# Holding back the third expert's search, moving half of a conversion to ScalarE, and pairing the experts in another way

## The chip, the cores and the metric

The kernel runs on one core of one Trainium2 chip. The metric is the device time of one execution in microseconds, the median of three runs. The core has five engines with a queue of instructions each: TensorE (PE) multiplies matrices, VectorE (DVE), ScalarE (ACT) and GpSimd (POOL) work on tiles in on-chip memory, and SyncE (SP) issues most transfers. Each queue runs in the order in which the program wrote it; an instruction that waits holds up all that is behind it on its engine.

## The reference

Three steps in a row: attention over 4 x 8 heads of 576 tokens, a layer of eight experts to which tokens are assigned by their scores, and one dense layer with a squared ReLU.

```python
# attention: causal, with a bias from cumulated s; x is its output, 2304 tokens x 512
# experts: cap = 288 tokens each
logits = x @ w_gate
order = np.argsort(-logits.flatten())
for idx in order:                      # best scores first
    tok, e = idx // E, idx % E
    if assigned[tok] >= 0 or counts[e] >= cap:
        continue
    assigned[tok] = e
    counts[e] += 1
for e in range(E):
    mask = assigned == e
    out[mask] = np.maximum(x[mask] @ w1[e], 0.0) @ w2[e]
# dense layer, 512 -> 2048 -> 512, its weights given in float64
h = np.maximum(out @ w_in, 0.0)
y = h * h @ w_out
```

## The kernel before

**Stages.** Attention runs first (to about 230 us). Then the eight experts are found one after the other. Each of eight searches (`route_phases`, one phase for each expert) finds by counting the threshold at which an expert has its 288 tokens, and then the tokens' numbers (`idxs`). A search is a chain of small steps between VectorE and TensorE: VectorE compares (`wide`, L573), TensorE counts (L690, L697), VectorE reads the count (`ev` L694, `ge` L703), TensorE spreads the answer (L706). At its end TensorE makes the indices (L770), and GpSimd gathers the expert's rows (`rows`, L1023).

**Experts and layers.** Expert `e` has two kinds of blocks on TensorE, eight of each: kind 1 (`h` from w1, then `hH` on ScalarE, `hL` on VectorE) and kind 2 (`acc`, from w2), twelve matmuls of 288 columns each. `CHUNKS` groups the experts; behind the last expert of a chunk its dense layers run, 16 blocks each of kind 3 (`h` from w_in, then `s`, `sH` on ScalarE, `s` squared on VectorE, `sL` on GpSimd) and kind 4 (`acc`, w_out). A pair has matmuls of 512 columns, a single expert has half the columns in kind 3 and half the matmuls in kind 4. All products are made of three matmuls of high and low parts; so each weight is split, `wH` on ScalarE and `wL` on GpSimd or VectorE (L990, L993), three blocks ahead (`LS`). At the end of a chunk GpSimd scatters the output rows (L1229), 128 at a time.

**Conversion.** w_in and w_out come as float64. `Convert` makes float32 of 128 columns at a time: `begin` makes the exponent and mantissa (`ex`; for w_in, n of 16 and above, on ScalarE, L862) and one 16-bit half of `sg` (L877, on VectorE), `begin2` the other half (L877), `end` puts them together (L888, VectorE). There is one buffer `sg`, three of `ex` and three of the raw words. All of w_out is converted beside attention, three pieces of w_in are begun in the first search, and the others, in every second block from block 18 on (`CV0`, `CVM`): they are needed from the first chunk's layers on. Converted pieces are split into `winH` (ScalarE) and `winL` (GpSimd).

**Order.** The loop over `order` in `experts` writes all queues by hand. After each block `wait` goes down by the block's cost (1.0 for an expert's block, 1.7 for a pair's layer block, 0.9 for a single expert's); once it is at or below zero one search step is written and `wait` rises by the step's weight times `YS` (0.5, up to the second expert's search) or `YL` (1.3, from then on). Block 16 is the first of the second expert. Rows of an expert that is second in its pair are gathered at once when its indices are there; rows of others one block after another.

Of the kernel before, what the change touches and what calls it, by code (L numbers as in the profile page):

```python
# [6 lines left out]
FT = mybir.dt.float32  # L7
# [3 lines left out]
U16 = mybir.dt.uint16  # L11
AF = mybir.ActivationFunctionType
OP = mybir.AluOpType
# [458 lines left out]
NTOK, DM, E_, F1, F2 = 2304, 512, 8, 1024, 2048  # L472
# [113 lines left out]
def route_begin(tc, cn, L):  # L586
    V = tc.nc.vector
    alive = cn.rp.tile([128, NT], FT, name="alive", bufs=1)
    V.memset(alive, 1.0)
    for b in range(B):  # L590
        V.memset(alive[64:128, 5 * b:5 * b + 1], 0.0)
    cn.alive = alive

    cn.wide = cn.rp.tile([128, 64 * NT], BF, name="wide", bufs=1)
    tc.nc.gpsimd.memset(cn.wide, 0.0)

    cn.oh = cn.rp.tile([128, GT * NG, 8], BF, name="oh", bufs=1)
    V.memset(cn.oh, 0.0)
    cn.front = Front(tc, cn, L, alive)
# [188 lines left out]

NB1, NB2 = F1 // 128, F2 // 128

CHUNKS = [[0, 1], [2, 3], [4, 5], [6], [7]]
LASTC = len(CHUNKS) - 1
W20 = 'SV'
W2X = 'SV'
# [2 lines left out]
RS = 1  # L797
# [6 lines left out]
YS = 0.5  # L804
GD = 1
GS = 2
YL = 1.3
ML = 3
RF = 8
GE = 2  # L810
# [12 lines left out]
class Convert:  # L823
# [25 lines left out]
    def begin(self, pool=False):  # L849
        n = self.begun  # L850
        if n >= self.loaded:
            return
        self.begun += 1
        hw = self.r64[n][:, :, :, 1]
        ex = self.cn.cv.tile([128, 4, 128], FT, name="ex", bufs=3)
        sg = self.cn.cv.tile([128, 4, 128], I32, name="sg", bufs=1)

        if pool:
            self.nc.gpsimd.tensor_tensor(ex, hw.bitcast(FT), self.cn.m112[:, :, None].to_broadcast([128, 4, 128]),
                                         op=OP.mult)  # L860
        else:
            self.nc.scalar.activation(ex, hw.bitcast(FT), AF.Copy, scale=2.0 ** -112)  # L862
        self.half(n, sg, 0, 13, OP.logical_shift_right)
        self.ex[n] = (ex, sg)

    def begin2(self):
        n = self.begun - 1
        if n < 0 or n in self.two:
            return
        self.two.add(n)  # L870
        self.half(n, self.ex[n][1], 1, 32768, OP.bitwise_and)

    def half(self, n, sg, k, x, op):

        u = self.r64[n].rearrange("p c f w -> p (c f w)").bitcast(U16).rearrange("p (f w) -> p f w", w=4)
        o = sg.rearrange("p c f -> p (c f)").bitcast(U16).rearrange("p (f w) -> p f w", w=2)
        self.nc.vector.tensor_scalar(o[:, :, k], u[:, :, 2 * k + 1], x, None, op0=op)  # L877

    def end(self):
        n = self.done  # L880
# [43 lines left out]
def early_pools(tc, cn, L, win, wout):  # L924

    nc = tc.nc
    pools = []

    def pool(name, bufs, **kw):
        p = tc.tile_pool(name=name, bufs=bufs, **kw)  # L930
        pools.append(p)
        return p.__enter__()

    cn.rp = pool("m_rt", 2)
    cn.cv = pool("m_cv", 2)
    fx = pool("m_cf", 1)
    cn.woutR = fx.tile([128, NB2, DM], FT, name="woutR")
    cn.m112 = fx.tile([128, 1], FT, name="m112")
    nc.vector.memset(cn.m112, 2.0 ** -112)
    route_begin(tc, cn, L)  # L940
    cn.conv = Convert(tc, cn, win, wout)
    return pools


def experts(tc, cn, L, xd, w1, w2, win, wout, out):
    nc = tc.nc
# [3 lines left out]
    def pool(name, bufs, **kw):  # L950
        p = tc.tile_pool(name=name, bufs=bufs, **kw)
        pools.append(p)
        return p.__enter__()
# [3 lines left out]
    fx = pool("m_fix", 1)  # L957
# [43 lines left out]
    eids, idxs = [], []  # L1001
    route = route_phases(tc, cn, L, cn.rp, rps, eids, idxs)
    wait = [0]

    def route_step():
        l0 = len(idxs)
        y = next(route, 0)

        return y
# [37 lines left out]
    def w_load(blk):  # L1047
        k, e, f = blk
        if k == 1:
            RAWS[blk] = raw(w1[bass.ds(ereg(e), 1)].rearrange("e (c p) f -> p (e c) f", p=128)  # L1050
                            [:, :, 128 * f:128 * f + 128])
        elif k == 2:
            RAWS[blk] = raw(w2[bass.ds(ereg(e), 1), 128 * f:128 * f + 128, :].rearrange("e p (c d) -> (e p) c d", c=4))

    def w_split(blk):
        k, e, f = blk
        if k in (1, 2):
            W[blk] = split(RAWS.pop(blk), "SG" if k == 1 else (W2X if e else W20))
        elif k == 4:
            W[blk] = split(woutR[:, f, :].rearrange("p (c d) -> p c d", c=4), WO if e else WO0)  # L1060
# [8 lines left out]
    def block(blk, mid=lambda: None):  # L1069
# [10 lines left out]
        elif k == 3:  # L1080
# [6 lines left out]
            h = ps.tile([128, 512], FT, name="h", bufs=2)  # L1087
            if len(CHUNKS[e]) == 2:

                o, yh, yl = h.rearrange("p (a n) -> p a n", a=2), *(  # L1090
                    y.rearrange("p d (a n) -> p d a n", a=2)[:, :, :, :256] for y in (yh, yl))
            else:
                o, yh, yl = h[:, :n], yh[:, :, :n], yl[:, :, :n]
            if f == 0 and len(CHUNKS[e]) == 2:

# [56 lines left out]
    def post2(e, a):  # L1152
        c = min(n for n, es in enumerate(CHUNKS) if e in es)
        off = CAP * CHUNKS[c].index(e)
        if c not in Y:
            ytile(c)
        yh, yl = (t[:, :, off:off + CAP] for t in Y[c])
        for d in range(4):
            S.activation(yh[:, d, :], a[d][:, :CAP], AF.Copy)
            V.tensor_tensor(yl[:, d, :], a[d][:, :CAP], f32(yh[:, d, :]), op=OP.subtract)  # L1160
        n = (e + 1) % E_
        V.tensor_copy(idxR[32 * (n % 4):32 * (n % 4) + 32, n // 4:n // 4 + 1], idxs[e][0:32, 2:3])
        if e not in CHUNKS[0] and e < E_ - 1:
            keep(e)

    def keep(e):
        c = min(n for n, es in enumerate(CHUNKS) if e in es)
        o = CAP * CHUNKS[c].index(e) + 256
        for r, y in zip(R, Y[c]):
            G.tensor_copy(r[:, :, 32 * e:32 * e + 32], y[:, :, o:o + 32])  # L1170
# [97 lines left out]
    while not idxs:  # L1268
        y = route_step()
# [13 lines left out]
    def need(e):  # L1283
        if lw[0] is None:
            xrows(99)
            late_stores(nc, cn, 0)
            cn.otp.__exit__(None, None, None)
            lw[0] = pool("m_lw", 2, side="right")
        while len(idxs) <= e:

            route_step()
        if e not in gathered:
            gathered.add(e)
            if e and [e - 1, e] in CHUNKS:

                for c in range(3):
                    gather(e, c)
                soon.extend((xt, (e, d), 0) for d in range(4))
                return
            for c in range(3):  # L1300
                if e >= GE:
                    gathers.append((e, c, at[0] + GD + GS * c))
                else:
                    gather(e, c)
            for d in range(4):
                side.append((xt, (e, d), at[0] + (GD + 2 * GS if e >= GE else 0) + SD))
# [33 lines left out]
    for n, blk in enumerate(order):  # L1340
        at[0] = n
        routed = False
        while nl < min(len(order), n + LD + 1):
            if order[nl][0] in (1, 2):
                need(order[nl][1])
            w_load(order[nl])
            nl += 1
        while ns < min(len(order), n + LS + 1):
            w_split(order[ns])
            ns += 1  # L1350
        if blk[0] == 1:
            while any(a[0] == blk[1] for f, a, _ in soon):
                xt(*soon.popleft()[1])
            while any(f is xt and a[0] == blk[1] for f, a, _ in side):
                side_step()

        block(blk, mid if len(idxs) < 2 else lambda: None)
        seen.add(blk)
        wait[0] -= cost(blk)
        turn = blk[0] == 2 and blk[2] == NB1 - 1 and (blk[1] < TE or len(idxs) == E_)  # L1360
        if turn:
            flush()
        if len(idxs) < E_ and wait[0] <= 0 and n >= RS:
            wait[0] += route_step() * (YL if len(idxs) > 1 else YS)
            routed = True
        flush()
        if conv.done < 2 * NB2 and n % CVM == CVO and n >= CV0:
            conv_step()
        while gathers and gathers[0][2] <= n:
            gather(*gathers.popleft()[:2])  # L1370

        k, e, f = blk
        if k > 2:
            e = CHUNKS[e][-1]
        for _ in range(2):
            if soon and (1, soon[0][1][0] - 1, NB1 - 1) in seen:
                xt(*soon.popleft()[1])
        for _ in range(1 if len(idxs) < E_ else SW):
            if side and side[0][2] + (0 if routed or len(idxs) == E_ else SL) <= n and not (
                    side[0][0] is xt and side[0][1][0] and (1, side[0][1][0] - 1, NB1 - 1) not in seen):  # L1380
                side_step()
        if k > 1 and e + 1 < E_ and len(idxs) > e + 1:
            need(e + 1)
# [50 lines left out]
```

## Time and profile before

| | us |
|---|---|
| median of three runs | 965.55 (965.05 to 967.3) |
| profiled execution, device time | 963.51 |
| its span, first to last instruction | 961.7 |
| TensorE busy | 898.0 |
| VectorE busy | 575.1 |
| ScalarE busy | 455.8 |
| GpSimd busy | 405.7 |

By the trace the stages lie as follows, in us from the span's start: attention to 230, first search 230 to 269, experts 0 and 1 from 269.5 to 346.6, layers of the pair 0 and 1 to 451.3, experts 2 and 3 to 514.8, their layers to 612.8, experts 4 and 5 to 674.4, their layers to 766, expert 6 to 792.1, its layers to 837.4, expert 7 to 864.3, its layers and the last stores to the end. Times below are read in these stages: the busy time of an engine in a stretch, and the waits, which name the engine that sat idle and the instruction that ended its idle time.

### The profile page before, as it was taken

To read this page: it belongs to the slowest core of one execution; us is meant where nothing else is said; L and a number is where in the kernel's file an instruction comes from. 1 tells how busy PE (TensorE), PEld (TensorE's weight loads), DVE (VectorE), ACT (ScalarE), POOL (GpSimd) and SP (SyncE) were. 2 spreads that over 40 slices of the span, in tenths; PEclk is the share of its full clock that TensorE was granted. 3 is DMA by queue.
4 is the path that set the end of the run, shared out by engine and by line. 5 is a ranking of instruction groups with operands and counts; after the bars stand their busy time and mean duration, and the time that the engine had idled before them with its cause. 6 is when DMAs were issued, how large, how long until landed. Compare 5 with 4: busy or idle time off the path is not lost.

```text
span 961.7 us, 16567 instructions
## 1 busy us (share of the span) xinstructions
PE 898.0 (93%) x5836; PEld 733.9 (76%) x5836; DVE 575.1 (60%) x1517; ACT 455.8 (47%) x1055; POOL 405.7 (42%) x330
## 2 busy tenths in 40 slices
PE   4999999998688798999999999989999999999996
PEld 3676767776478786777898777889888899898885
DVE  7787888887867988734756444756432344442222
ACT  6677767775334554233353233443432455553321
POOL 4454554443523656646442321633323454533233
PEclk9999999999589999999999999999999999999999
DMA  6877696733634632101641100455000160140001
GB/s 169 212 175 191 152 241 169 189 96 124 202 104 136 204 103 77 33 1 45 208 133 44 33 1 1 136 150 164 13 1 1 49 204 1 29 137 1 0 1 45
DMA packets 73971, 95.54 MB, mean 99 GB/s; under 512 B 8128, under 2 KB 53184, under 8 KB 73888
## 3 DMA queue, kind: packets, MB, share of 16 engines
q1 hardware_dynamic: 68560, 79.93, 30.4%
q0 software_dynamic: 3360, 11.01, 3.4%
q10 hardware_dynamic: 1968, 3.54, 1.0%
q8 instruction: 46, 0.75, 0.3%
q14 instruction: 37, 0.30, 0.1%
HBM read 80.31 MB, written 9.44 MB: 93 GB/s over the span
## 4 chain that ended last, share of the span: by engine, by line
PE 74%; DVE 14%; issue 4%; DMA 4%; POOL 2%; ACT 2%; SPq 0%; DVEq 0%; POOLq 0%; ACTq 0%
PE h L1065 10%; PE h L1067 9%; PE h L1066 9%; PE acc L1113 6%; PE acc L1114 6%; PE acc L1115 6%; PE av L271 5%; PE pt L244 5%; PE acc L1065 3%; PE acc L1067 3%; PE acc L1066 3%; PE sc L199 3%; DVE sg L877 2%; DVE Q L168 2%; PE sc L200 2%
## 5 line engine op out<-in xcount | busy, mean ns | idle before, releaser
L1180 POOL TENSOR_TENSOR sL<-s,sH 128x512 fp32r<-128x512 f32 (+1 forms) x80 | 111.6, 1394 | 252.0 <-DVE s L1179 245.3
L1175 ACT ACTIVATE s<-h 128x512 f32<-128x512 f32 (+1 forms) x80 | 44.5, 556 | 220.7 <-PE h L1067 220.6
L1179 DVE TENSOR_TENSOR s<-s 128x512 f32<-128x512 f32 (+1 forms) x80 | 53.3, 667 | 153.0 <-ACT sH L1178 152.8
L993 POOL TENSOR_TENSOR wL<-raw,wH 128x512 fp32r<-128x512 f32 x64 | 83.5, 1312 | 98.4 <-ACT wH L990 96.2
L1065 PE MATMUL h<-yH,winH 128*128 128x512 f32 (+1 forms) x332 | 124.1, 374 | 0.0
L1067 PE MATMUL h<-yH,winL 128*128 128x512 f32 (+1 forms) x332 | 121.2, 365 | 0.0
L1066 PE MATMUL h<-yL,winH 128*128 128x512 f32 (+1 forms) x332 | 121.0, 364 | 0.0
L1113 PE MATMUL acc<-wH,sH 128*128 128x512 f32 x288 | 116.3, 404 | 0.0
L990 ACT ACTIVATE wH<-raw 128x512 fp32r<-128x512 f32 x128 | 80.2, 629 | 76.0 <-DMA raw<-in_w 39.8
L1114 PE MATMUL acc<-wL,sH 128*128 128x512 f32 x288 | 113.5, 394 | 0.0
L1115 PE MATMUL acc<-wH,sL 128*128 128x512 f32 x288 | 113.5, 394 | 0.0
L227 ACT ACTIVATE e<-sc,nm 128x576 f32<-128x576 f32 (+4 forms) x160 | 84.1, 526 | 48.1 <-DVE junk L216 41.4
L216 DVE TENSOR_SCALAR_CACHE_REDUCE junk<-sc 128x576 bf16<-128x576 f32 (+4 forms) x160 | 77.6, 485 | 34.0 <-PE sc L202 25.7
L244 PE MATMUL pt<-ident,e 128*128 128x128 f32 x448 | 81.4, 288 | 5.3 <-ACT e L227 4.8
L199 PE MATMUL sc<-K,Q 128*128 128x288 f32 (+2 forms) x192 | 74.0, 390 | 10.5 <-DVE Q L152 10.5
L1065 PE MATMUL h<-xH,wH 128*128 128x288 f32 x256 | 81.0, 316 | 2.7 <-DVE hL L1143 2.7
L1065 PE MATMUL acc<-hH,wH 128*128 128x288 f32 x256 | 79.1, 309 | 0.0
L1066 PE MATMUL h<-xL,wH 128*128 128x288 f32 x256 | 77.0, 301 | 0.0
L1067 PE MATMUL h<-xH,wL 128*128 128x288 f32 x256 | 76.4, 299 | 0.1
L1067 PE MATMUL acc<-hH,wL 128*128 128x288 f32 x256 | 75.8, 296 | 0.0
L1066 PE MATMUL acc<-hL,wH 128*128 128x288 f32 x256 | 75.7, 296 | 0.0
L160 POOL TENSOR_TENSOR K<-k,K 64x1152 fp32r<-64x1152 f32 x15 | 39.7, 2648 | 78.8 <-DMA q<-in_qT 21.9
(225 smaller groups left out, 2107.4 us busy)
## 6 DMA issues: line engine op xcount, KB each, us to landing
raw<-in_w SPq DMA_DIRECT2D x128, 256.0 KB
k<-in_kT SPq DMA_DIRECT2D x30, 288.0 KB
q<-in_qT SPq DMA_DIRECT2D x30, 288.0 KB
r<-in_wout SPq DMA_DIRECT2D x16, 512.0 KB
r<-in_win SPq DMA_DIRECT2D x16, 512.0 KB
vb<-in_vm SPq DMA_DIRECT2D x16, 256.0 KB
Q<-Q SPq DMA_DIRECT2D x8, 288.0 KB
QB<-Q SPq DMA_DIRECT2D x7, 288.0 KB
```

The source lines that it names most:

```text
L199: nc.tensor.matmul(o, Q1[:, a, c0:c0 + 128], K1[:, a, x0:x1], start=True, stop=False)
L227: nc.scalar.activation(o, v, AF.Exp, bias=nm[:m], scale=0.125, accum_out=sums[b % 2][:m, i, hd % H:hd % H + 1])
L244: nc.tensor.transpose(pt[:, j, :m], (E4[hd % 2] if i == 4 else E[i])[:m, 128 * j:128 * j + 128], cn.ident[:m, :m])
L990: S.activation(hi, src, AF.Copy)
L993: (G if eng[1] == "G" else V).tensor_tensor(lo, src, f32(hi), op=OP.subtract)
L1065: T.matmul(o, wh, xh, start=first, stop=False)
L1066: T.matmul(o, wh, xl, start=False, stop=False)
L1067: T.matmul(o, wl, xh, start=False, stop=last)
L1113: T.matmul(o, hi[:, c0:c0 + 128], wh, start=f == 0, stop=False)
L1114: T.matmul(o, hi[:, c0:c0 + 128], wl, start=False, stop=False)
L1115: T.matmul(o, lo[:, c0:c0 + 128], wh, start=False, stop=f == NB2 - 1)
L1180: G.tensor_tensor(lo, s, f32(hi), op=OP.subtract)
```

## The change

Four things change. The chunks are `[0, 1], [2], [3, 4], [5, 6], [7]` in place of `[0, 1], [2, 3], [4, 5], [6], [7]`. The third expert's search (two sets of indices are there) isn't written before block 26 (`R2`), in the middle of the second expert, and `wait` doesn't sink below -1. The weight of a search step is taken from a table, 1.2 and 1.25 in place of 1.3. And of the conversion of w_in one half of `sg` is made on ScalarE, as a product with 2^-13 and an added constant whose rounding gives the shift.

```diff
-CHUNKS = [[0, 1], [2, 3], [4, 5], [6], [7]]
+CHUNKS = [[0, 1], [2], [3, 4], [5, 6], [7]]
...
-YL = 1.3
+YY = [0, 0.5, 1.2, 1.2, 1.2, 1.25, 1.25, 1.25]
+R2 = 26
...
-        self.half(n, sg, 0, 13, OP.logical_shift_right)
+        o, u = self.halves(n, sg)
+        if n < NB2:
+            self.nc.vector.tensor_scalar(o[:, :, 0], u[:, :, 1], 13, None, op0=OP.logical_shift_right)
+        else:
+
+            self.nc.scalar.activation(o[:, :, 0], u[:, :, 1], AF.Identity, bias=self.cn.mhalf, scale=2.0 ** -13)
...
-        self.half(n, self.ex[n][1], 1, 32768, OP.bitwise_and)
...
+        o, u = self.halves(n, self.ex[n][1])
+        self.nc.vector.tensor_scalar(o[:, :, 1], u[:, :, 3], 32768, None, op0=OP.bitwise_and)
...
+    nc.vector.memset(cn.mhalf, -0.5 + 2.0 ** -14)
...
-        if len(idxs) < E_ and wait[0] <= 0 and n >= RS:
-            wait[0] += route_step() * (YL if len(idxs) > 1 else YS)
+        if len(idxs) < E_ and wait[0] <= 0 and n >= (R2 if len(idxs) == 2 else RS):
+            y = YY[len(idxs)]
+            wait[0] = max(wait[0], -1.0) + route_step() * y
```

The lines below the new ones move by 6 to 9: L862 becomes L863, L888 becomes L894, L993 becomes L1001, L1023 becomes L1031, L1143 becomes L1151, L1229 becomes L1237.

VectorE's queue in the second expert, beside its conversions; first before, with pieces of the third search (`k2f`, `wide`, `base`, `ev`, `ge`) between them:

```order
L573 TENSOR_TENSOR wide<-thr,k2f 128x840
L678 SCALAR_TENSOR_TENSOR base<-mi,base 128x1
L1143 SCALAR_TENSOR_TENSOR hL<-h,hH 128x288
L888 SCALAR_TENSOR_TENSOR ex<-ex,sg 128x512
L877 TENSOR_SCALAR sg<-r_4453 128x512 x2
L993 TENSOR_TENSOR wL<-raw,wH 128x512
L1143 SCALAR_TENSOR_TENSOR hL<-h,hH 128x288
L888 SCALAR_TENSOR_TENSOR ex<-ex,sg 128x512
L877 TENSOR_SCALAR sg<-r_4518 128x512 x2
L694 CAST ev<-mi 128x24
L993 TENSOR_TENSOR wL<-raw,wH 128x512
L703 TENSOR_SCALAR ge,some<-mi 42x8
```

and after:

```order
L1151 SCALAR_TENSOR_TENSOR hL<-h,hH 128x288
L894 SCALAR_TENSOR_TENSOR ex<-ex,sg 128x512
L878 TENSOR_SCALAR sg<-r_3394 128x512
L1001 TENSOR_TENSOR wL<-raw,wH 128x512
L1151 SCALAR_TENSOR_TENSOR hL<-h,hH 128x288
L894 SCALAR_TENSOR_TENSOR ex<-ex,sg 128x512
L878 TENSOR_SCALAR sg<-r_3527 128x512
L1001 TENSOR_TENSOR wL<-raw,wH 128x512
```

One L878 stands where two L877 stood, and for four conversions no search row stands between them.

ScalarE's queue at the same place after the change (`r` are the raw words):

```order
L1150 ACTIVATE hH<-h 128x288
L998 ACTIVATE winH<-ex 128x4x128
L863 ACTIVATE ex<-r_3527 128x512
L869 ACTIVATE sg<-r_3527,mhalf 128x512
L998 ACTIVATE wH<-raw 128x512 x2
L1150 ACTIVATE hH<-h 128x288
```

L869 is new in each such group of two blocks; the other rows stood there before too.

GpSimd's queue behind the layers of the first pair, where the third expert begins; before:

```order
L1229 DMA out<-r_5749,idx 2304x512
L1228 MEMSET spacer 1x1
L1229 DMA out<-ex,idx 2304x512
L993 TENSOR_TENSOR wL<-raw,wH 128x512
L1228 MEMSET spacer 1x1
L1229 DMA out<-ex,idx 2304x512
L1023 DMA rows<-xd,idx 128x512 x3
L993 TENSOR_TENSOR wL<-raw,wH 128x512 x6
```

and after:

```order
L1237 DMA out<-r_5649,idx 2304x512
L1001 TENSOR_TENSOR wL<-raw,wH 128x512
L1236 MEMSET spacer 1x1
L1237 DMA out<-ex,idx 2304x512
L1236 MEMSET spacer 1x1
L1237 DMA out<-ex,idx 2304x512
L1001 TENSOR_TENSOR wL<-raw,wH 128x512 x3
```

The three gathers of the fourth expert's rows have left this place for the single expert's layers. Behind those layers two scatters now stand, and the fifth expert's three gathers four weight splits later; behind the layers of experts 3 and 4 there are four scatters with three gathers among them, as there were behind those of 2 and 3.

## Rows read from the trace of the kernel before

**Rows 1.** The page, part 1: TensorE's busy time, share and instructions.
```profile
PE 898.0 (93%) x5836; PEld 733.9 (76%) x5836; DVE 575.1 (60%) x1517; ACT 455.8 (47%) x1055; POOL 405.7 (42%) x330
```

**Rows 2.** Stretches: length, then busy us (instructions) of PE, PEld, DVE, ACT, POOL; PEclk; DMA.
```profile
766.00:792.10 26.10, 26.10 (x198) 26.07 (x197) 11.95 (x20) 12.67 (x27) 13.61 (x15) 1.00 0.71 217
792.10:837.40 45.30, 45.30 (x298) 41.19 (x297) 20.76 (x39) 24.79 (x56) 19.73 (x20) 1.00 0.00 1
317.00:346.60 29.60, 23.27 (x178) 21.86 (x176) 28.35 (x54) 15.79 (x31) 15.76 (x11) 0.94 0.56 171
346.60:397.00 50.40, 45.42 (x237) 34.99 (x236) 45.47 (x82) 22.85 (x40) 34.14 (x24) 1.00 0.23 69
451.30:514.80 63.50, 59.68 (x485) 56.10 (x485) 42.29 (x130) 27.20 (x56) 24.38 (x25) 1.00 0.47 142
514.80:612.80 98.00, 98.00 (x521) 75.73 (x520) 53.63 (x146) 33.03 (x59) 30.57 (x26) 1.00 0.08 22
```

**Rows 3.** Waits of TensorE, 317 to 346.6: total us, times, longest.
```profile
PE mi L697 <- DVE ev L694: 4.9, 3, 3.5
PE mi L706 <- DVE ge L703: 1.4, 1, 1.4
```

**Rows 4.** Waits of TensorE, 346.6 to 400.
```profile
PE mi L690 <- DVE wide L573: 2.7, 2, 2.2
PE mi L770 <- DVE wide L763: 2.3, 1, 2.3
```

**Rows 5.** Waits of TensorE, 400 to 900, the longest three.
```profile
PE h L1065 <- DVE hL L1143: 2.7, 2, 1.8
PE mi L690 <- DVE wide L573: 2.6, 1, 2.6
PE mi L706 <- DVE ge L703: 1.2, 1, 1.2
```

**Rows 6.** VectorE in order of time from 328.4: start, us, engine, line, operation.
```profile
328.58 0.81 DVE L877 TENSOR_SCALAR sg<-r 128x512 uint16<-128x512 uint16 x2
...
331.70 2.82 DVE L877 TENSOR_SCALAR sg<-r 128x512 uint16<-128x512 uint16 x2
334.42 0.16 DVE L694 CAST ev<-mi 128x24 f16<-128x24 f32 x1
```

**Rows 7.** GpSimd in order of time, the same stretch.
```profile
331.06 1.73 POOL L993 TENSOR_TENSOR wL<-raw,wH 128x512 fp32r<-128x512 f32 x1
332.76 1.45 POOL L993 TENSOR_TENSOR winL<-ex,winH 128x512 fp32r<-128x512 f32 x1
```

**Rows 8.** VectorE in order of time from 359: a compare of the search.
```profile
362.46 1.44 DVE L573 TENSOR_TENSOR wide<-thr,k2f 128x840 bf16<-128x840 bf16 x1
```

**Rows 9.** Line L877 alone in two stretches: length, busy us (instructions).
```profile
317.00:346.60 29.60, 10.64 (x14) 0.94 0.56 171
346.60:397.00 50.40, 16.15 (x12) 1.00 0.23 69
```

**Rows 10.** Order of time from 234: a conversion's half in the first search.
```profile
234.11 1.30 DVE L877 TENSOR_SCALAR sg<-r 128x512 uint16<-128x512 uint16 x1
235.30 0.14 DVE L703 TENSOR_SCALAR_CACHE_REDUCE ge<-mi 42x8 bf16<-42x8 f32 x1
...
235.51 0.16 PE L706 MATMUL mi<-some,onesb 42*128 42x1 bf16 x1 [1.99 <-DVE ge L703]
```

**Rows 11.** ScalarE's groups, 317 to 346.6: busy us, mean ns of one | idle before.
```profile
L990 ACT ACTIVATE wH<-raw 128x512 fp32r<-128x512 f32 x10 | 6.2, 628 | 5.5 <-PE acc L1066 2.6 <-DMA raw<-in_w 2.3 <-PE acc L1067 0.5
L862 ACT ACTIVATE ex<-r 128x512 f32<-128x512 f32 x6 | 4.0, 666 | 0.5 <-POOL winL L993 0.5
...
L1142 ACT ACTIVATE hH<-h 128x288 fp32r<-128x288 f32 x5 | 2.0, 408 | 5.1 <-PE h L1067 5.1
```

**Rows 12.** TensorE in order of time from 294.9: second expert's indices, then its rows.
```profile
295.30 0.47 PE L770 MATMUL mi<-vv,wide 128*128 128x6 bf16 x10
...
303.50 0.66 PE L1032 MATMUL mi<-ident,rows 128*128 128x128 f32 x4 [1.43 <-DMA rows<-xd,idx]
```

## What the change was predicted to do

> **What bounds the kernel now.** I read the page first: TensorE is busy for 93% of the span [rows 1]. Its work is the same before and after (the same matmuls in another order), so all that a change of order can win is TensorE's idle time and what holds it up. I then cut the span into the stages of the experts and read how full each was [rows 2]. Sixteen blocks of an expert take 26.1 us where nothing disturbs them (766 to 792), 1.63 us a block. The second expert and the first pair's layers are not full: TensorE is busy for 23.27 of 29.60 us from 317 to 346.6, and for 45.42 of 50.40 us from there to 397. In both VectorE has hardly a free moment (28.35 and 45.47 us). From 514.8 to 612.8 a search runs as well and TensorE never idles; there no conversion runs.
>
> The view of waits says what TensorE waited for. From 317 to 346.6 it waited 6.3 us, all for answers of the search (`ev`, `ge`) from VectorE [rows 3]. In the next 50 us it waited 5.0 us, again for the search (`wide`) [rows 4]. From 400 to 900 its three longest groups make 6.5 us [rows 5]. Why VectorE is late shows in time order: a search answer of 0.16 us at 334.42 stands behind two halves of a conversion that took 2.82 us together, while the pair at 328.58 took 0.81 us [rows 6]. Between 331.06 and 334.21 GpSimd ran two instructions without a gap, and the two halves ended 0.3 us behind them [rows 7]. All in all the halves (L877) cost VectorE 10.64 us over 14 in the first stretch and 16.15 us over 12 in the second, 0.76 and 1.35 us each [rows 9].
>
> **The change, part by part.** The sum is made on the profiled execution: span 961.7 us, device time 963.51 us, which is 2.04 us below the median of the three runs shown, 965.55 us. Gains are carried over to the median as they are.
>
> *One half of each conversion of w_in on ScalarE, in the first search.* Three of the sixteen conversions start there. One of the halves that go stands at 234.11, takes 1.30 us, and the search's `ge` starts only behind it, at 235.30, for which TensorE idled 1.99 us [rows 10]. Without it `ge` can start at about 234.2: 1.1 us. For the other two I count from nothing to the 0.4 us that a half takes undisturbed (0.81 / 2); ScalarE gets three instructions more, but is off this chain. Taken: 0.9 us; bounds 0 and 1.1 + 2 x 0.4 = 1.9.
>
> *The second expert, 317 to 346.6.* Two things leave VectorE: the search (held until block 26) and seven of fourteen halves, 7 x 0.76 = 5.3 us. The 6.3 us of waits all end in search answers, so their places are gone; also TensorE's granted clock was 0.94 on average there, which is the lower level for 12% of 29.6 us, so up to 1.8 us of work was lost, and it was 1.00 in every later stage of [rows 2]; I take 1.0 of it. What is late next: ScalarE now does in each pair of blocks one `hH`, one `winH`, one `ex`, two `wH` and the moved half. By [rows 11] that was 0.41 + 0.67 + 3 x 0.63 = 2.97 us, with `winH` taken as a `wH`, which has its shape; the new instruction has no row, and its nearest one is `ex`, the same 512 elements of the same tile: 0.67 us, in all 3.64 us against 3.26 us for two blocks of TensorE. Over seven pairs ScalarE falls behind by 2.7 us, part of which the weight splits, made three blocks ahead, absorb. The moved half also waits for L894 on VectorE, since there is one buffer `sg`; queued behind it on ScalarE are the two `wH`, which have those three blocks of time, and the next `hH`, which has not. I leave 2.0 us of new waits, between 0 and 6. Gain 6.3 + 1.0 - 2.0 = 5.3 us; bounds 0.3 and 8.1.
>
> For the price of the moved half, ScalarE: Activation LUTs (the Trainium skill, section What ACT_TABLE_LOAD costs) states 280 ns + 0.833 ns an element where the bias is a pointer, an estimate of 0.71 us for it. By it ScalarE would be 7 x 0.04 = 0.3 us later here; no row of before has this instruction.
>
> *The first pair's layers, 346.6 to 397.* Six of twelve halves go, 6 x 1.35 = 8.1 us of VectorE's 45.47. The search runs there in about the same density as before (a step for each 1.2 cost units, before 1.3), but earlier in its course. The two long waits, 2.2 and 2.3 us [rows 4], are each longer than one half of 1.4 us; with a half less in the queue they would be 0.8 and 0.9 us, and the small third one 0. Gain 3.3 us; bounds 0 (the waits move to other steps) and 5.0.
>
> *Third expert alone, later.* TensorE's work is the same: the single expert's layers cost 45.30 us [rows 2] wherever they stand. What moves are the edges, where one chunk's layers end and the next expert begins. (a) At the first edge `hL` came late, 1.8 of the 2.7 us in [rows 5]. It stays, and nine transposes of the third expert's rows now stand directly ahead of its first block: 2.5 us. (b) GpSimd's queue of four output scatters and three gathers in a row made weights late; I put down to it 1.2 us at the first edge (the `ge` of [rows 5]) and 2.6 us at the next. Now the first edge has no gather in it, the third one has: 2.6 us. (c) The fifth expert's rows come late: TensorE has four blocks, 6.5 us, between its last index matmul and the transposes. The second expert's gather before took from 295.30 to 303.50, 8.2 us, and TensorE waited 1.43 us [rows 12]. I take 1.7 us. (d) The fifth search runs beside the single layers, whose blocks are 1.4 us long (45.30 / 32) and had no search before; the nearest stage with a search and short blocks is 451.3 to 514.8, where TensorE idled 3.8 us [rows 2]. I take 2.0 us, between 0 and 6. (e) 0.9 us at the last expert's edge, as before. After the change 2.5 + 2.6 + 1.7 + 2.0 + 0.9 = 9.7 us against 6.5: a loss of 3.2 us, between a gain of 2 and a loss of 8.
>
> Sum: 0.9 + 5.3 + 3.3 - 3.2 = 6.3 us. The profiled execution would take 957.2 us, the median **959.2 us**.
>
> **The rivals.** *A: ScalarE becomes the bound in the second expert.* If the 0.38 us by which it exceeds two blocks is not absorbed, and each moved half waits half a microsecond for L894, seven pairs lose 7 x 0.88 = 6.2 us, and the stage gains 1.1 instead of 5.3: 963.4 us. For it: 3.64 against 3.26 us. Against: ScalarE idled 5.5 us ahead of its splits in that stretch [rows 11], and splits run ahead.
>
> *B: the wait for GpSimd passes to the next instruction.* A half costs 0.4 us alone and 1.4 us beside GpSimd. If the remaining half, or the compare behind it, then waits in its place, the halves that went freed only their 0.4 us, 13 x 0.4 = 5.2 us of VectorE instead of 13.4, and the waits of the held search reappear in the layers: 0.5 + 4.0 (second expert) + 0.5 - 3.2 = 1.8 us, 963.8 us. SBUF - State Buffer (the Trainium skill, section Who interferes with whom) states that the two engines share one port pair and that the one that issues later fully blocks until the other's instruction ends. By that rule the next VectorE instruction of such a form blocks, as in B; the trace agrees as far as L877 goes, 2.82 against 0.81 us [rows 6]. Against B: two halves blocked in turn on two instructions of GpSimd, and a single one can block on one only.
>
> *C, slower: answers don't come back within a short block.* In the single layers TensorE asks for a search answer after 1.4 us. If the compare takes the 1.44 us of [rows 8] and an `s` stands ahead of it, each of some 12 steps there costs 0.8 to 1.0 us and the fifth expert's gather 3 us more: (d) becomes 12, (c) 4.7. That is 13 us worse than the forecast: 972.2 us. It decides from the point at which an answer takes longer than a block; at half of it the result is no change. Against it: expert blocks of 1.63 us carry such steps with 3.8 us lost in 63.5.
>
> *D: the hold isn't one.* The order shows four conversions of the second expert on VectorE with no search row between them, so it does what it says; 0.
>
> **How the numbers follow.** Forecast 58%, A 15%, B 13%, C 14% (half of which ends at no change or a small loss). The forecast's own bounds are 952 to 964: 7 us better if nothing is lost at the edges and in the second expert alike, 5 us worse if one of the two goes wrong. To leave out no more than 2 in 10, the range takes in A, B and the near part of C: 952 to 967. A measurement of this kernel can tell 0.2%, 1.9 us, from no change. Faster by more: the forecast, half of A and of B, which lie at the edge of it: 0.72. Within it: the other half of both and a little of C: 0.16. Slower: the rest of C: 0.12.
>
> **What would show it.** Right: the second expert from its first conversion to the layers shrinks from 29.6 to some 24 us, with no wait for `ev` or `ge` until its last blocks; waits for `wide` in the layers' first 50 us of 1 to 2 us; in the first search `ge` straight behind `z`; a wait for the fifth expert's rows of 1 to 3 us. Wrong: waits for ScalarE's `hH` (A), moved halves gone but L878 at 1.4 us or more with the same waits behind it (B), or waits of 1 us in every second block of the third expert's layers (C).

## The result and the profile after

The changed kernel takes **974.22 us** (median, 968.59 to 977.3) against 964.86 us of the kernel before (961.8 to 967.3): ratio 1.009, 95% interval 1.0065 to 1.0116. It is slower by 9.4 us where 6.3 us of gain were forecast. The profiled execution of after has a span of 974.8 us (before 961.7).

By the two profiles TensorE did the same matmuls and was busy 12.4 us longer, idle only 0.7 us longer. This is the row of the page that answers to [rows 1]:

```profile
PE 910.4 (93%) x5836; PEld 742.5 (76%) x5836; DVE 557.8 (57%) x1502; ACT 465.2 (48%) x1071; POOL 400.7 (41%) x330
```

VectorE lost 17 us of work and ScalarE got 9, as meant. The busy time grew where the clock was low. The stages of after, as in [rows 2] (stretch, length, busy us of PE, PEld, DVE, ACT, POOL, then PEclk, DMA): experts 0 and 1, their layers, expert 2, its layers, experts 3 and 4, their layers, experts 5 and 6.

```profile
268.70:347.60 78.90, 67.30 (x474) 61.16 (x473) 53.30 (x127) 39.42 (x78) 31.77 (x24) 0.91 0.48 142
347.60:451.40 103.80, 100.01 (x522) 76.17 (x520) 59.84 (x140) 46.20 (x82) 62.78 (x51) 0.99 0.16 48
451.40:482.40 31.00, 31.00 (x229) 29.63 (x228) 15.81 (x48) 11.59 (x24) 11.30 (x13) 0.91 0.49 144
482.40:535.30 52.90, 52.07 (x377) 44.71 (x376) 34.81 (x102) 25.50 (x58) 20.89 (x23) 1.00 0.06 17
535.30:600.00 64.70, 60.49 (x475) 57.05 (x474) 39.47 (x115) 27.27 (x57) 24.61 (x24) 0.97 0.48 139
600.00:698.80 98.80, 98.80 (x521) 75.57 (x520) 45.96 (x134) 32.96 (x59) 29.59 (x24) 1.00 0.08 22
698.80:761.40 62.60, 57.94 (x448) 56.71 (x447) 35.36 (x81) 27.83 (x59) 27.67 (x29) 0.95 0.56 169
```

Four stages show a PEclk more than a hundredth under 1.00, and in three of them an expert's rows or indices come in. Before, every stage behind 346.6 was at 1.00 (five of the six stretches of [rows 2] lie there). To add this up I split the stretch from the first expert's first block to the last expert's layers into three: idle time of TensorE (length less busy time), what the lower clock of 1.2 GHz cost (half of the busy time granted 0.50), and the rest, work at 2.4 GHz. It is worked out from the trace's intervals of TensorE and its record of the clock, in us:

| kernel | length | idle | lower clock | work |
|---|---|---|---|---|
| before | 594.8 | 23.5 | 4.2 | 567.1 |
| after | 608.1 | 25.1 | 14.1 | 568.9 |
| after, waits filled (e8) | 600.7 | 16.6 | 6.5 | 577.6 |
| after, two `sg` (e1) | 598.8 | 19.7 | 10.4 | 568.6 |
| after, no hold (e4) | 597.7 | 21.7 | 7.5 | 568.5 |
| after, two `sg`, no hold (e5) | 586.2 | 16.2 | 2.3 | 567.7 |
| before, hold alone (e10) | 606.6 | 27.9 | 9.7 | 569.0 |

Of the 13.3 us between before and after, 9.9 are the lower clock, 1.6 idle time and 1.8 work. These are two single executions, and they lie further apart than the kernels do: after's has the lowest mean granted clock of its ten (0.960, the others up to 0.973). Span times what the mean clock lacks to 1, averaged over all runs, is 32.6 us for after and 26.6 to 28.2 for the kernel before in the groups below, so an estimate for the clock's part of the 9.4 us between the medians is 4 to 6 us. The row of e5 is the fastest of its ten runs, 5.8 us under their median.

Two places decide the time: the second expert, where the gain that was forecast didn't come, and the edges, where 12.4 us were lost.

**The second expert.** From 317 to 347.6 VectorE is no longer full (23.60 of 30.60 us; 28.35 of 29.60 before [rows 2]) and one wait of 0.7 us is left for the search, yet the stage did not shrink. The waits there name a new pair of engines (total us, times, longest; other lines between them left out):

```profile
ACT sg L869 <- DVE ex L894: 11.5, 5, 3.4
...
POOL wL L1001 <- ACT wH L998: 6.7, 4, 2.1
DVE wL L1001 <- ACT wH L998: 6.1, 5, 1.6
...
PE h L1075 <- POOL wL L1001: 2.6, 3, 0.9
```

In order of time (start, us, engine, line), ScalarE first, then VectorE, then what TensorE waits for:

```profile
322.31 0.88 ACT L869 ACTIVATE sg<-r,mhalf 128x512 uint16<-128x512 uint16 x1 [1.83 <-DVE ex L894]
323.06 1.12 ACT L998 ACTIVATE wH<-raw 128x512 fp32r<-128x512 f32 x2
...
327.41 0.88 ACT L869 ACTIVATE sg<-r,mhalf 128x512 uint16<-128x512 uint16 x1 [1.84 <-DVE ex L894]
```

```profile
324.21 1.40 DVE L1001 TENSOR_TENSOR wL<-raw,wH 128x512 fp32r<-128x512 f32 x1 [1.50 <-ACT wH L998]
325.54 0.45 DVE L1151 SCALAR_TENSOR_TENSOR hL<-h,hH 128x288 fp32r<-128x288 f32 x1
325.90 1.41 DVE L894 SCALAR_TENSOR_TENSOR ex<-ex,sg 128x512 int32<-128x512 int32 x1
327.35 0.48 DVE L878 TENSOR_SCALAR sg<-r 128x512 uint16<-128x512 uint16 x1
```

```profile
325.12 0.40 PE L1075 MATMUL h<-xH,wL 128*128 128x288 f32 x1 [0.88 <-POOL wL L1001]
...
328.81 0.40 PE L1073 MATMUL h<-xH,wH 128*128 128x288 f32 x1 [0.50 <-ACT wH L998]
...
330.21 0.40 PE L1075 MATMUL h<-xH,wL 128*128 128x288 f32 x1 [0.87 <-POOL wL L1001]
```

It is a circle. The moved half (L869) waits 1.84 us until `end` (L894) has read the only `sg`; the two `wH` behind it on ScalarE wait with it; VectorE's `wL` waits for `wH`; and the next L894 is queued behind that `wL`. One turn serves two blocks and takes 327.41 - 322.31 = 5.1 us, where two undisturbed blocks take 3.26. No engine is full in it. Two of its steps, `wL` (1.40) and L894 (1.41), ran while GpSimd made splits too; by themselves each takes 0.69 us elsewhere in this trace, so some 1.4 us of the turn (an estimate) come with GpSimd.

**The edges.** Three long waits of TensorE lie where an expert begins or ends its search (a wait in brackets; all three on TensorE, from three places):

```profile
450.87 0.90 PE L1040 MATMUL mi<-ident,rows 128*128 128x128 f32 x3 [2.58 <-DVE xL L1051]
...
560.41 0.33 PE L1040 MATMUL mi<-ident,rows 128*128 128x128 f32 x1 [1.11 <-DMA rows<-xd,idx]
562.12 0.66 PE L1040 MATMUL mi<-ident,rows 128*128 128x128 f32 x4 [1.38 <-DMA rows<-xd,idx]
...
721.24 0.70 PE L770 MATMUL mi<-vv,wide 128*128 128x6 bf16 x10 [3.49 <-DVE wide L763]
```

Stretches right behind them (columns as above):

```profile
451.40:458.20 6.80, 6.80 (x39) 6.73 (x38) 1.86 (x6) 2.18 (x5) 2.34 (x4) 0.59 0.21 44
...
562.80:566.20 3.40, 3.40 (x16) 3.38 (x16) 0.82 (x2) 0.94 (x3) 1.28 (x1) 0.50 0.07 19
...
721.80:726.60 4.80, 4.80 (x25) 4.80 (x23) 2.58 (x6) 0.93 (x2) 0.00 (x0) 0.50 0.36 108
```

TensorE never idles there, but half as fast: a clock of 0.50 is 1.2 GHz. By the record of the clock the lower stretches begin at 450.1, 562.8 and 719.8 and last 6.8, 3.4 and 6.8 us. In this execution each of the three waits is thus paid a second time.

### The profile page after: what moved, and what is told of

It reads as the page before. It is cut to its first block, busy times and chain, and to the rows that moved or that the text cites. A ratio compares the mean times of both kernels' runs of the same rounds, so it can differ in the third digit from the quotient of the medians.

```text
span 974.8 us, 16582 instructions
## 1 busy us (share of the span) xinstructions
PE 910.4 (93%) x5836; PEld 742.5 (76%) x5836; DVE 557.8 (57%) x1502; ACT 465.2 (48%) x1071; POOL 400.7 (41%) x330
## 4 chain that ended last, share of the span: by engine, by line
PE 76%; DVE 11%; DMA 4%; issue 3%; ACT 2%; POOL 2%; SPq 0%; DVEq 0%; POOLq 0%; ACTq 0%
PE h L1073 10%; PE h L1074 9%; PE h L1075 9%; PE acc L1121 7%; PE acc L1123 6%; PE acc L1122 6%; PE pt L244 5%; PE av L271 5%; PE acc L1073 3%; PE acc L1074 3%; PE acc L1075 3%; PE sc L199 3%; PE sc L200 2%; DVE Q L168 2%; DVE wide L573 1%
## 5 line engine op out<-in xcount | busy, mean ns | idle before, releaser
L1188 POOL TENSOR_TENSOR sL<-s,sH 128x512 fp32r<-128x512 f32 (+1 forms) x80 | 108.9, 1361 | 255.6 <-DVE s L1187 226.7
L1001 POOL TENSOR_TENSOR wL<-raw,wH 128x512 fp32r<-128x512 f32 x64 | 82.8, 1299 | 112.9 <-ACT wH L998 109.8
L1073 PE MATMUL acc<-hH,wH 128*128 128x288 f32 x256 | 81.2, 317 | 1.4 <-ACT wH L998 1.4
L1075 PE MATMUL acc<-hH,wL 128*128 128x288 f32 x256 | 78.2, 305 | 0.2 <-DVE wL L1001 0.2
L1074 PE MATMUL acc<-hL,wH 128*128 128x288 f32 x256 | 78.3, 306 | 0.0
```

Source lines behind the costliest of these rows:

```text
L1001: (G if eng[1] == "G" else V).tensor_tensor(lo, src, f32(hi), op=OP.subtract)
L1073: T.matmul(o, wh, xh, start=first, stop=False)
L1074: T.matmul(o, wh, xl, start=False, stop=False)
L1075: T.matmul(o, wl, xh, start=False, stop=last)
L1188: G.tensor_tensor(lo, s, f32(hi), op=OP.subtract)
```

## The experiments

The runs came in four groups, each beside runs of the kernel before on its own chip (medians 964.3 to 964.4). Theories: **T1**, the circle through the one `sg` costs the second expert its gain; **T2**, the new chunks cost it; **T3**, the hold brings all later searches late to the edges, and the clock doubles each wait. "Stage" times run from a stage's first to its last block.

**e1: a second buffer for `sg`.** There is no room for it beside four `hH` and `hL`, so these get three.

```diff
-        sg = self.cn.cv.tile([128, 4, 128], I32, name="sg", bufs=1)
+        sg = self.cn.cv.tile([128, 4, 128], I32, name="sg", bufs=2)
...
-        hi = wk.tile([128, CAP], FR, name="hH", bufs=4)
-        lo = wk.tile([128, CAP], FR, name="hL", bufs=4)
+        hi = wk.tile([128, CAP], FR, name="hH", bufs=3)
+        lo = wk.tile([128, CAP], FR, name="hL", bufs=3)
```

> The changed kernel with two buffers sg in place of one (the space comes from three hH and hL in place of four). Theory 1 (a loop through the one buffer: the moved half on ScalarE waits for L894, the two wH wait behind it, VectorE's wL waits for wH, hL and L894 stand behind wL; 5.1 us for two blocks that TensorE does in 3.3): L869 waits no more, the second expert from 317 to its layers takes 24 to 27 us instead of 30.4, experts 0 and 1 together 73 to 76 us instead of 78.9, the drop of the clock at 341 goes; time 966 to 970. Theory 2 (the edges of the new chunks cost it all): experts 0 and 1 shorter by 2 us at most, time 972 to 975.

Measured: 967.08 us, ratio to before 1.004 (1.002 to 1.0059), 7.1 us below after. Experts 0 and 1 went from 78.9 to 72.2 us, every other stage stayed within 1.1 us. The drop of the clock at the end of the second expert, which was expected to go, stayed (6.8 us from 333.5). ScalarE in time order shows the circle open, the half comes 4.2 us after the last one with no wait in front:

```profile
316.80 0.87 ACT L869 ACTIVATE sg<-r,mhalf 128x512 uint16<-128x512 uint16 x1
...
321.00 0.87 ACT L869 ACTIVATE sg<-r,mhalf 128x512 uint16<-128x512 uint16 x1
```

T1 is shown, for 7 us. The kernel is still not faster than before.

**e2: the old chunks**, all else as after.

```diff
-CHUNKS = [[0, 1], [2], [3, 4], [5, 6], [7]]
+CHUNKS = [[0, 1], [2, 3], [4, 5], [6], [7]]
```

> The changed kernel with the chunks of before ([0, 1], [2, 3], [4, 5], [6], [7]). Theory 2 (the edges: transposes of the third expert's rows directly ahead of its first block, the fifth expert's gather that comes late, the clock that falls behind each): the stretch behind 451 is 10 to 13 us shorter, time 961 to 965. Theory 1 (the loop in the second expert): that stretch is the same within 4 us, time 970 to 974.

Measured: 971.32 us, ratio 1.0095 (1.0057 to 1.0132). T2 falls as the main cause: the old chunks give back 2.9 us, less than these four runs can tell. Most of what they keep is in one row, experts 2 and 3 (63.50 us before [rows 2]), again with a clock below 1:

```profile
449.00:517.80 68.80, 62.12 (x498) 58.16 (x496) 41.77 (x125) 27.02 (x57) 25.18 (x26) 0.95 0.41 127
```

**e3: both halves on VectorE again**, all else as after.

```diff
-        if n < NB2:
+        if True:
```

> The changed kernel with both halves of the conversion on VectorE, as before. Theory 1: L869 and its wait are gone, but VectorE has 1.4 us more for each two blocks beside hL, L894 and wL, about 5.1 us again: experts 0 and 1 take 76 to 79 us, time 972 to 976. If VectorE were not in the loop, 73 us and 968.

Measured: 974.79 us, ratio 1.0108 (1.0082 to 1.0134), like after. The two stages at issue:

```profile
271.70:344.60 72.90, 64.81 (x475) 59.53 (x474) 56.86 (x133) 36.20 (x75) 32.69 (x24) 0.92 0.51 154
344.60:452.40 107.80, 102.12 (x521) 77.82 (x520) 65.99 (x147) 40.84 (x72) 63.05 (x50) 0.97 0.15 46
```

The circle is gone (72.9, not the 76 to 79 expected), but the layers take 107.8 instead of 103.8, where the same halves take VectorE's time again. So the moved half is worth 4 us in the layers and costs 6 in the second expert.

**e4: no hold**, all else as after.

```diff
-R2 = 26
+R2 = 1
```

> The changed kernel without the hold (R2 = 1): the third search runs through the second expert again. Theory 2: the third expert's indices come some 30 us earlier, its transposes don't stand ahead of its first block, the wait of 2.6 us at 448 and the drop of the clock at 450 (3.4 us) go: 968 to 971, if the second expert doesn't get longer. Theory 1: the search is added to the loop in the second expert, experts 0 and 1 take 80 us or more, and the rest wins less than that: 973 to 977.

Measured: 965.39 us, ratio 1.0011 (0.999 to 1.0032), better than either theory allowed. Experts 0 and 1 take 79.3 us, as in after, though they now hold a search as well; experts 5 and 6 take 55.4 instead of 62.6, at full clock:

```profile
695.50:750.90 55.40, 53.45 (x404) 52.93 (x402) 22.96 (x46) 27.62 (x59) 27.67 (x28) 1.00 0.64 191
```

The last indices were there before that stage. This is what made T3.

**e5: two `sg` and no hold** (the edits of e1 and e4).

> The kernel after with the hold taken out (R2 = 1) and a second buffer sg (hH and hL have three buffers in place of four). The kernel after with two sg alone took 967.1 us and without the hold alone 965.4, against 974.2. If the loop through one sg and the hold cost time apart from one another, both gains add up: 974.2 - 7.1 - 8.8 = 958 us, and experts 0 and 1 take 73 to 75 us. If the search that the hold moves had only filled TensorE's idle time that the loop makes, then with the loop gone its work comes to light: experts 0 and 1 take 77 to 79 us and the kernel 963 to 966.

Measured: **959.65 us** (953.9 to 962.96), ratio 0.9955 (0.9936 to 0.9974): faster than before and after. The two gains (7.1 and 8.8) add up to within 1.5 us. The second expert with a search in it takes no longer than without (72.4 against 72.2 in e1):

```profile
268.20:340.60 72.40, 64.67 (x508) 59.32 (x508) 58.96 (x155) 41.08 (x81) 31.47 (x24) 0.97 0.51 158
...
683.60:738.90 55.30, 53.44 (x402) 52.90 (x401) 23.95 (x45) 27.55 (x59) 27.68 (x28) 1.00 0.63 191
```

**e6: on the kernel before, the moved half and two `sg` alone** (the change's edits in `begin` and `begin2`, and those of e1; no new chunks, hold or weights).

> The kernel before with the moved half alone and a second buffer sg (hH and hL have three buffers in place of four): old chunks, no hold, weights 0.5 and 1.3. If the new chunks cost time by themselves (the edge in front of the third expert), this is 3 us or more below the run with new chunks, two sg and no hold, and at 956 to 959 us. If the chunks cost nothing without the hold, the two agree within 2 us.

Measured: 960.26 us, ratio 0.9965 (0.9944 to 0.9986), 0.6 us from e5. So in this setting old and new chunks (with their weights) can't be told apart, and all the gain there is comes from the conversion.

**e7: on the kernel before, the new chunks alone.**

> The kernel before with the new chunks alone. If the third expert alone costs what the prediction gave its edges, 3.2 us, it takes 967 to 969 us against 964.4 of the kernel before. If the edges became dear only because the held search brought the later ones there late, it takes 963 to 966.

Measured: 967.71 us, ratio 1.0036 (1.0017 to 1.0055): 3.4 us more, where the prediction had put 3.2 on its edges. With e6 in mind this is a cost of the setting, not of the chunks as such. Where the 3.4 us lie is not shown: its profile is of the lowest of its runs (962.03 us, below the kernel before). In it the single expert's layers with a search never idle, which speaks against rival C:

```profile
482.00:532.10 50.10, 50.10 (x365) 43.38 (x364) 34.69 (x103) 25.03 (x57) 15.05 (x20) 1.00 0.01 1
```

**e8: the waits filled.** The kernel after, with matmuls nobody reads queued ahead of the three waits.

```diff
+            if lastp and t0 == n:
+                for _ in range(FIX):
+                    nc.tensor.matmul(ix, cn.onesb, cn.onesb[:, None, :].to_broadcast([128, 4, 128]),
+                                     start=True, stop=True)
...
+FILL = {(2, 2): 11, (4, 0): 10}
+FIX = 15
...
+            if (e, d) in FILL:
+                for _ in range(FILL[e, d]):
+                    T.matmul(ps.tile([128, 512], FT, name="h", bufs=2), cn.onesb,
+                             cn.onesb[:, None, :].to_broadcast([128, 4, 128]), start=True, stop=True)
```

> The kernel after with 36 matmuls of 128x512 whose results nobody reads, queued on TensorE at three places where it waited: 11 ahead of the third expert's seventh transpose (2.58 us of wait), 10 ahead of the fifth expert's transposes (1.11 + 1.38 us) and 15 ahead of the last indices (3.49 us). They take some 0.21 us each. If the lower clock of the 3.4 to 6.8 us behind each wait comes from the wait, it is gone there (granted clock 1.00 from 450 to 457, 563 to 566 and 720 to 727), and the kernel takes 5 to 7 us less, 967 to 969 us, though it does more. If the clock falls for another reason, or the waits only move, it takes 973 to 976 us and the lower stretches stay.

Measured: 968.55 us, ratio 1.0043 (1.0027 to 1.0059), 5.7 us below after, with 36 matmuls more. The fillers ahead of the last indices, which then come without a wait, and the stretches behind the three places:

```profile
710.64 3.41 PE L769 MATMUL mi<-onesb 128*128 128x512 bf16 x15
713.88 0.40 PE L774 MATMUL mi<-vv,wide 128*128 128x6 bf16 x10
```

```profile
448.30:455.00 6.70, 6.70 (x59) 6.44 (x57) 3.46 (x10) 3.21 (x7) 3.45 (x6) 1.00 0.36 113
...
560.00:564.00 4.00, 4.00 (x38) 3.75 (x37) 2.42 (x11) 3.13 (x7) 2.95 (x4) 1.00 0.46 134
...
718.00:724.00 6.00, 6.00 (x50) 6.00 (x49) 2.70 (x6) 3.04 (x9) 1.83 (x2) 1.00 0.41 116
```

All three lower stretches are gone, and the mean clock over the ten runs is 0.9718 against 0.9665 of after: here the lower clock came with TensorE's idling at the edge.

**e9: hold kept, quicker searches.** The kernel after with weights 1.0 from the fourth search on.

```diff
-YY = [0, 0.5, 1.2, 1.2, 1.2, 1.25, 1.25, 1.25]
+YY = [0, 0.5, 1.2, 1.0, 1.0, 1.0, 1.0, 1.0]
```

> The kernel after with the hold and one sg, but weights 1.0 in place of 1.2 and 1.25 from the fourth search on, so that the last indices come behind 664 groups of matmuls and not behind 728; the sixth expert begins behind 672. If the hold costs time because it brings the later searches late to the edges (the fifth expert's rows, the last indices beside scatters and gathers), experts 5 and 6 take 55 to 57 us in place of 62.6, experts 3 and 4 60 to 62 in place of 64.7, and the kernel 963 to 967. If what counts is that the second expert's idle time isn't used by a search any more, nothing changes: 972 to 975.

Measured: 967.83 us, ratio 1.0031 (1.0016 to 1.0047): 6.4 us below after, just short of the expectation. Experts 5 and 6 take 55.5 us, 3 and 4 62.1. But the third expert's layers rose from 52.9 to 58.0, since now the fifth search ends on their last block and TensorE waits there for its compares:

```profile
481.30:539.30 58.00, 54.30 (x389) 45.91 (x388) 40.08 (x111) 25.65 (x59) 22.35 (x26) 0.97 0.10 28
```

```profile
PE mi L770 <- DVE wide L763: 3.7, 2, 2.5
```

**e10: on the kernel before, the hold alone.**

```diff
+R2 = 26
...
-        if len(idxs) < E_ and wait[0] <= 0 and n >= RS:
-            wait[0] += route_step() * (YL if len(idxs) > 1 else YS)
+        if len(idxs) < E_ and wait[0] <= 0 and n >= (R2 if len(idxs) == 2 else RS):
+            wait[0] = max(wait[0], -1.0) + route_step() * (YL if len(idxs) > 1 else YS)
```

> The kernel before with the hold alone (chunks, both halves on VectorE and the weight 1.3 as before). By the prediction's step the waits for the search in the second expert go, and most of 5.3 us is gained: 958 to 961. If the hold only brings the searches late, experts 0 and 1 take 72 to 74 us (77.1 before), the pair's layers 107 (104.7) and experts 2 and 3 68 to 69 (63.5), as in the run with the old chunks and the hold: 967 to 970.

Measured: 977.15 us, ratio 1.0116 (1.0096 to 1.0137): 12.9 us more, above both expectations and 3 us slower than the whole change. Experts 0 and 1 shrink to 73.3, the layers take 108.0, and experts 2 and 3 take 72.5 (63.5 before; 4.4 us more of it idle time, 4.8 lower clock). There the fourth search is not done when its expert's weights must be asked for, and its last steps run one behind another, each with a wait; then TensorE waits for the rows:

```profile
478.82 0.19 PE L738 MATMUL mi<-prb,upper 128*128 128x40 bf16 x1 [1.29 <-DVE prb L729]
...
481.16 0.70 PE L770 MATMUL mi<-vv,wide 128*128 128x6 bf16 x10 [1.87 <-DVE wide L763]
...
488.74 0.33 PE L1033 MATMUL mi<-ident,rows 128*128 128x128 f32 x1 [1.34 <-DMA rows<-xd,idx]
```

**e11: on the kernel before, the moved half alone**, one `sg`.

> The kernel before with the moved half alone and one sg. If the half that moves frees VectorE, as the prediction's second and third step have it, the kernel takes 958 to 961. If the loop through the one sg takes back in the second expert what is won in the layers, experts 0 and 1 take 78 to 80 us, the layers 102 to 103, and the kernel 963 to 966, some 4 us above the run with two sg (960.3).

Measured: 965.25 us, ratio 1.0003 (0.9984 to 1.0022): no change, as T1 has it, 5.0 us above e6. The layers take 102.5, as expected; experts 0 and 1 76.1, not the 78 to 80 expected. The circle is there: L869 waits 10.0 us for L894 in five times, its first full turns take 5.1 us, and in e6 it doesn't wait at all. But experts 0 and 1 take 75.0 us in e6's profile, so of the 5.0 us between the medians the profiles show 1.1 in that stage.

**e12: the kernel after with both remedies**, two `sg` and the weights of e9.

> The kernel after with both remedies: two sg (hH and hL have three buffers in place of four) and weights 1.0 from the fourth search on; the hold stays. If the loop and the late searches are the two causes and don't depend on one another, 974.2 less 7.1 (two sg) less what the quicker searches gain (8 to 9): 958 to 960, like the run with two sg and no hold (959.7). If the hold costs something beyond these, it stays 3 us or more above that run.

Measured: 963.61 us, ratio 0.9979 (0.9964 to 0.9995), 4.0 us above e5. The third expert's layers take 57.7 us, as in e9. Whether those 4 us are the hold's or that edge's was left to two more runs.

**e13 and e14: the search's end moved off that edge** by weights 0.9 for the fourth and fifth search, with two `sg` (e13) and one (e14).

```diff
-YY = [0, 0.5, 1.2, 1.2, 1.2, 1.25, 1.25, 1.25]
+YY = [0, 0.5, 1.2, 0.9, 0.9, 1.0, 1.0, 1.0]
```

> As the run with two sg and weights 1.0, but weights 0.9 for the fourth and fifth search: the fifth expert's indices come behind 408 groups of matmuls in place of 420, the third expert's layers end behind 416. If the 4 us are the search's end on the edge, these layers take 52 to 53 us in place of 57.7 and the kernel 958 to 961. If the hold costs them by itself, or the denser search costs as much in the short blocks (rival C of the prediction), it stays at 963 to 965.

Measured: 961.16 us, ratio 0.9964 (0.9945 to 0.9983), and 54.3 us for the layers, idle for 0.7; both lie just above what the edge alone would give:

```profile
472.60:526.90 54.30, 53.62 (x390) 44.90 (x389) 39.34 (x125) 25.54 (x58) 18.84 (x21) 1.00 0.04 11
```

> The same weights with one sg, the kernel after with nothing but its weights changed. If the search's end on the edge is the cost, 967.8 (weights 1.0) less 4 to 5: 962 to 965. If not, 967 to 969.

Measured: 966.75 us, ratio 1.0019 (0.9995 to 1.0044), between the two expectations: 1.1 us below e9, with an interval of 2 us on either side. With two `sg`, 2.5 of the 4 us went by the medians, about as much as these runs can tell, and 3.4 in these layers by the profiles: the edge was the larger part. The 1.5 us between e13 and e5 are less than these runs can tell.

Five pairs of these kernels differ in the second `sg` alone (with its three `hH` and `hL`): after and e1, e4 and e5, e11 and e6, e9 and e12, e14 and e13. It was worth 7.1, 5.7, 5.0, 4.2 and 5.6 us.

## Why the prediction was wrong

By the two profiles the kernel lost 13 us where the sum had 6.3 to gain. Experts 0 and 1 were 7.1 us worse than the sum, the edges 9.2, the first pair's layers 2.4. So two terms failed: the new waits in the second expert, and the edges, for which the later ends of the held search and the clock were not in the sum.

**First search: not to be told.** Predicted 0.9 us. In after the first expert begins 0.8 us earlier (268.7 against 269.5) and TensorE's waits for `ge` fell from 4.4 to 2.2 us, while those for compares rose from 0.7 to 3.2: part of the wait moved on, as rival B had it, and all waits of the first search together are 14.1 us against 14.0. Over all profiles the time from the search's first count to the first expert is 36.1 to 38.0 us with the moved half and 37.1 to 37.9 without, so a gain under 1 us doesn't stand out.

**The second expert: this step failed.** A gain of 5.3 us was predicted, the stage became 1.8 us longer. The waits for the search went, as said, but for 0.7 of 6.3 us. The mis-sized term is "2.0 us of new waits, between 0 and 6": TensorE's waits for `wH` and `wL` in that stretch add up to 5.2 us, within the bounds. With it the clock went the other way: 1.0 us was to come back, and over experts 0 and 1 the lower clock cost 2.5 us more (6.7 against 4.2). The mechanism was named (the moved half waits for L894, with `wH` and `hH` queued behind it) and so was a price, 0.5 us a pair in rival A; the moved half waited 1.83 us and more, 11.5 us in five pairs. The error was to count ScalarE's busy time against two blocks, 3.64 to 3.26 us, as if the weights' three blocks of lead could cover a wait that comes again in every pair. It is a circle through two engines and one buffer, and its turn of 5.1 us sets the pace whatever the lead. The instruction itself took 0.88 us, not the 0.67 of its nearest row. By the price that ScalarE: Activation LUTs (the Trainium skill, section What ACT_TABLE_LOAD costs) states, the estimate was 0.71 us; the measurement decides, 0.88.

**First pair's layers: right in its waits.** TensorE waits 1.2 us to 400, where it was 5.0 [rows 4], 1.7 left by the prediction. The stage gained only 0.9, since the wait of 2.58 us at its end, predicted as 2.5 at edge (a), lies in it. The half that is left on VectorE still takes 1.44 us there (L877 took 1.35 on average [rows 9]), as rival B had it, but the waits that B expected of it did not come.

**The edges: the waits right, their price wrong.** (a) 2.58 us for 2.5; (c) 1.11 + 1.38 = 2.5 for 1.7; (b) 3.49 for 2.6, but not by GpSimd's cluster alone, since a weight landed late (ScalarE waited 4.42 us for it) and the last search's steps stood behind it on VectorE; why it was late stays open. (d) 0.8 for 2.0: rival C did not come in after, and in e9 and e12 only where a search ended on the edge. (e) None for 0.9. Together 9.4 us for 9.7. Yet from 451.4 to the last layers after takes 425.4 us, before 413.0 (451.3 to 864.3): 12.4 us more, where the sum had 3.2 at all edges. Of these 7.1 are the lower clock (2.8, 1.7 and 2.6 behind the three waits), 2.4 idle time and 2.9 work. 1.1 of the work was done in earlier stages before (33 search matmuls stand here now); what the other 1.8 are stays open. The prediction counted the clock once, as a gain of 1.0 us in the second expert, and took the 1.00 of the later stages [rows 2] for granted. The length of a wait alone doesn't tell: the kernel before had one of 2.6 us [rows 5] with no lower stretch behind it, and the wait at the first edge, 2.6 us in e2 and e9 as in after, had none behind it there. So one profile is not a price for this term. What else decides stays open.

**The hold: its second end was not priced.** The prediction wrote what the hold takes away and not where the searches then end. Each of the five later searches moves with the third, so that the fifth expert's indices and the last ones fall on edges: the last come at 721 to 727 us in after, inside the stage of experts 5 and 6, and by 687 in e4, ahead of it. e10 shows the hold alone, 12.9 us; e4 (without it) gains 8.8 us and e9 (quicker searches) 6.4.

**The bounds.** 974.2 lies above the range's 967. The sum's own worst ends were 0.3 us of gain in the second expert and 8 us of loss at the edges; measured were 1.8 us of loss and 12.4. Rival C's 972.2 came nearest by a mechanism that was not there.

## What to carry to other kernels

Before an instruction is moved to another engine, follow its buffers: with one buffer that two engines write and read in turn, the move closes a circle whose turn, not the engines' busy time, sets the pace; price it as the sum of one turn, and see whether a second buffer fits (here worth 4.2 to 7.1 us in five pairs of kernels). Where something is held back in a chain, write down where the chain's later ends fall, and keep them off the places where other work waits. Waits of TensorE at the edges were paid twice in the profile of after, so a sum of waits must have a column for the clock behind them, and a few idle matmuls in such a place are a cheap test of it.

## What was not expected of the hardware

- The lower clock behind waits of 2.49 to 3.49 us, for 3.4 to 6.8 us each, and its absence when the same 8 us or so were filled with matmuls (e8). A wait of 2.2 us at the first edge of e5 was followed by no such stretch, nor was the one of 2.6 us at the first edge of e2 and e9.
- The moved half, 512 elements of 16 bits read at a distance, took ScalarE 0.88 us, against 0.67 for the same number of 32-bit elements (L863, same place, a product without an added constant). Which of the two differences costs the time is not shown.
- A lower stretch of the clock that begins between 20 and 27 us, in attention, which is the same in all these kernels, lasted 3.4 us in six of the 16 profiled executions and 13.7 in seven. The first search's first count then came at 229.8 to 232.4 us, and at 232.5 to 234.0. It shifts all that follows, so stages were compared from the first expert on.
